# Softmax steps from VectorE to GpSimd, other decoding scratch and a new first-block order in a convolution and gated-MLP kernel

## The chip, the core and the metric

The kernel runs on one core of a Trainium2 chip. The metric is the device time of one execution in microseconds (us). The kernel before took 734.68 us (median of three executions: 734.12, 734.68 and 738.72).

## What is computed

```python
# x (4, 4160, 192), weight_gen (4, 4160, 8, 7), moe_w_in (192, 1024), moe_conv_w (3, 1024), moe_w_out (1024, 192)
w = softmax(weight_gen, axis=-1)                    # 7 taps for each token and head, 1e-9 added to the sum
x_pad = 6 zero rows ahead of each sequence, then x
a[b, s, head h] = sum over k of w[b, s, h, k] * x_pad[b, s + k, head h]      # 8 heads of 24 channels
hid = relu(a @ w_in)                                # (4, 4160, 1024)
conv = conv_w[0] * hid[s - 1] + conv_w[1] * hid[s] + conv_w[2] * hid[s + 1]  # by channel, zeros outside
out = (hid * sigmoid(conv)) @ w_out                 # (4, 4160, 192), float32
```

The weights arrive as float64, so as pairs of 32-bit words; the kernel makes float32 of them itself (the decoding below).

## The kernel before, in words

**Tiling.** The 16640 tokens lie as 128 partitions of 130 consecutive tokens. A block is four tokens of every partition, 512 in all; there are 33 blocks, and the softmax weights are loaded and normalised for a group of two blocks at a time (17 groups; group 0 holds block 0 alone, so group g holds blocks 2g-1 and 2g).

**A block** passes through these stages. *Taps* (`tap`, L283): seven products of the rows in `ring` with the softmax weights `w`, four into a tile `px` and three into `py`. *Folds*: for blocks 3 and later a DMA on POOL's queue adds `py` onto `px` (`fold1`, L314), a second one adds half of `px` onto the rest (`fold2`, L317), and POOL adds the last two (`fold3`, L321). Blocks 0 to 2 skip the folds: their seven taps are transposed one by one and summed in PSUM, and `PLAN` says for each tap whether VectorE (V) or GpSimd (G) makes it. *Transposes* (`transposes`, L326): PE turns the 192 channels onto partitions, 128 in a first part and 64 in a second; both parts of a folded block go through the same PSUM bank, so the second waits until ACT (L337) and DVE (L342) have split the first into a high and a low float32r part. *Units*: eight per block (f = 0 to 7), each five matmuls (L358), then on ACT relu (L364) and the middle conv term (L368), on DVE the two side terms (L375), on ACT the tanh (L382), on DVE the gating product (L391). Five PSUM banks hold units. *Output*: four tiles per block (L404), each eight products of float32 (16 matmul records in the trace), copied by ACT (L413) and stored.

**Softmax** (`sm_ops`): maximum on DVE (L238), subtraction (L241), exp on ACT (L244), sum on DVE (L247), 1e-9 on ACT (L251), reciprocal on DVE (L256), product (L263). `SMX` names for each group the engine of the subtraction and of the product, and `SMR` those of the groups past its end.

**Decoding** at the start: `CH` has five chunks of the first weight matrix and `WOE` four of the output weights. Each takes two ACT copies of the raw words (L132, L135), a clamp, a shift, a sign and a join (L139 to L150), and for the first matrix a split (L586, L591). Its scratch is two buffers `scr` of three slots. A chunk of kind "f" (the last 64 channels) ends in scratch, from where eight DMAs in all, the *spreads* (L603), take it to `wi`; in the kernel before the third chunk writes the same slot of `scr` as the first.

**Order.** Every step is a task with a modelled duration; a list scheduler (L786 to L849) places all of them from priorities (`TO`, `FO`, `WO_`, `FORD`), and the program is written out in the order of the placed starts. So each engine runs a fixed order, and waits in it. Around a DVE step of kind "VK" the planner keeps POOL free: before the next POOL step DVE and POOL write a small `tok` tile (L860, L861), and POOL waits for DVE there.

Of the kernel before, what the change touches and what calls it, by code (L numbers as in the profile page):

```python
# [22 lines left out]
    ("a", "GVVGGGG"),  # L23
    ("a", "GGVGGGG"),
    ("a", "GVVGVGG"),
)
REST = ("d", G7)
SMX = ("VV", "VV", "VG", "VG", "VG", "GV", "GV", "GV", "VV", "VV", "VV")
SMR = "GG"
TO = -3.05  # L30
FO = -0.55
WO_ = 1.42
NX = 3
# [7 lines left out]
    ("f", 0, 256, 5.2, "VVS", "V"),  # L41
    ("m", 0, 256, 8.7, "VGS", "V"),
    ("f", 256, 512, 17.0, "VVP", "G"),
    ("m", 256, 512, 16.0, "VVP", "V"),
    ("m", 512, 1024, 18.0, "VVP", "V"),
)
FORD = (2, 3, 5, 7, 0, 6, 1, 4)
WOE = ("VVP", "VVP", "GVS", "GVS")

# [15 lines left out]
def kernel(  # L65
# [357 lines left out]
    with tc.manual_schedule():  # L423
# [38 lines left out]
        for j in range(2, WB):  # L462
            load_w(j)
        for c in range(4):
            nc.sync.dma_start(
                out=r_out[c].rearrange("p (c d) b -> p c (d b)", c=2),
                in_=w_out.bitcast(I32)[2 * c * P:2 * (c + 1) * P, :].rearrange("(c p) e -> p c e", p=P),
            )

        temps = [hrow(f, 0, R).bitcast(I32) for f in range(2)] + [t[:, i] for t in scr for i in range(3)]  # L470

# [34 lines left out]
        def arrive(t):  # L506
            return task("none", t, [])
# [64 lines left out]
        spreads = []  # L572
        w_rdy, free = {f: [] for f in range(NF)}, {0: [], 1: []}
        for c, (kind, a, b, t, eng, wle) in enumerate(CH):
            n = b - a
            tA, tB, tC = temps[2 + 3 * (c % 2):5 + 3 * (c % 2)]
            d3 = tA[:, 0:n]
            raw = (r_in if kind == "m" else r_fold)[:, a:b, :]
            pm = eng[2] == "P"
            j_, bits = dec(None if pm else d3, raw, tB[:, 0:n], tC[:, 0:n], arrive(t), free[c % 2], eng)  # L580
            if kind == "m":
# [13 lines left out]
            if kind == "m":  # L595
                for f in range(a // P, b // P):
                    w_rdy[f].append(b_)
            else:
                def spread(th=th, a=a, b=b, n=n):
                    for s_ in range(2):  # L600
                        for r in range(2):
                            c_ = s_ * FF // 2
                            nc.sync.dma_start(  # L603
                                out=wi[r * D2:(r + 1) * D2, :, 1, c_ + a:c_ + b].bitcast(F32),
                                in_=th[s_ * D2:(s_ + 1) * D2, :, 0:n].bitcast(F32),
                            )
                b_ = dma(2.6, [b_], spread)
                spreads.append(b_)
                for f in range(a // P, b // P):
                    w_rdy[f].append(b_)  # L610
                    w_rdy[f + NF // 2].append(b_)
            free[c % 2] = [b_]
        wo_rdy = []
        for c in range(4):
            w = 2 * D
            j_, _ = dec(
                wo[:, 2 * c:2 * c + 2].rearrange("p c d -> p (c d)").bitcast(I32), r_out[c],
                temps[2 + 3 * (c % 2)][:, 0:w], temps[3 + 3 * (c % 2)][:, 0:w], arrive(21.0 + 1.5 * c), free[c % 2], WOE[c],
            )
            free[c % 2] = [j_]  # L620
            wo_rdy.append(j_)
# [72 lines left out]
        def unit(j, f):  # L694
# [11 lines left out]
            t_ = task("A", act(m_) + 0.02, [cv_], lambda: sig(j, f))  # L706
            dep = [tiles[j - 2, i] for i in range(geom(j - 2)[0])] if j >= 2 else free[0] + free[1] if j else []
            rd[n] = gm[n] = task("V", vec(m_, 0), [t_] + dep, lambda: gmul(j, f))
# [185 lines left out]
```

## Time and profile before

| what | value |
|---|---|
| median of three executions | 734.68 us |
| profiled execution | 738.26 us, span 736.3 us |
| PE busy | 697.9 us (95% of the span) |
| DVE busy | 640.1 us (87%) |
| ACT busy | 547.3 us (74%) |
| POOL busy | 497.2 us (68%) |
| mean granted TensorE clock | 0.988 of full |

The span runs from the first to the last instruction of the profiled execution; its time is 1.96 us longer. Busy shares are means over the whole span: where PE stands still is seen only by place, in the timeline and in the list of waits. The profile's line numbers are those of the kernel before; the changed kernel has the same lines one further on up to L466, and 9 to 14 further on behind that.

### The profile page before, as it was taken

To read this page: it belongs to the slowest core of one execution; us is meant where nothing else is said; L and a number is where in the kernel's file an instruction comes from. 1 tells how busy PE (TensorE), PEld (TensorE's weight loads), DVE (VectorE), ACT (ScalarE), POOL (GpSimd) and SP (SyncE) were. 2 spreads that over 40 slices of the span, in tenths; PEclk is the share of its full clock that TensorE was granted. 3 is DMA by queue.
4 is the path that set the end of the run, shared out by engine and by line. 5 is a ranking of instruction groups with operands and counts; after the bars stand their busy time and mean duration, and the time that the engine had idled before them with its cause. 6 is when DMAs were issued, how large, how long until landed. Compare 5 with 4: busy or idle time off the path is not lost.

```text
span 736.3 us, 10944 instructions
## 1 busy us (share of the span) xinstructions
PE 697.9 (95%) x3809; PEld 633.6 (86%) x3809; DVE 640.1 (87%) x1000; ACT 547.3 (74%) x1049; POOL 497.2 (68%) x391
## 2 busy tenths in 40 slices
PE   1599999999979999999999999999899999999998
PEld 1477999998979999999988999999799999999998
DVE  6589999999999998989879897979988888888882
ACT  3278788777778877868778877868687777877872
POOL 3495987989677686787778787777767887630000
PEclk9899999999999999999999999999999999999999
DMA  7615999899988867989697977889687886782111
GB/s 228 175 37 141 208 229 199 182 237 205 228 184 201 182 180 182 204 180 210 164 214 155 207 191 183 186 193 208 161 194 165 190 184 163 168 175 80 64 51 44
DMA packets 70787, 127.59 MB, mean 173 GB/s; under 512 B 5046, under 2 KB 42573, under 8 KB 70732
## 3 DMA queue, kind: packets, MB, share of 16 engines
q0 software_dynamic: 20160, 58.99, 45.5%
q1 hardware_dynamic: 50090, 67.51, 28.2%
q8 instruction: 30, 0.49, 0.3%
q10 hardware_dynamic: 482, 0.40, 0.2%
q14 instruction: 25, 0.20, 0.1%
HBM read 20.51 MB, written 12.78 MB: 45 GB/s over the span
## 4 chain that ended last, share of the span: by engine, by line
PE 28%; DMA 27%; POOL 26%; DVE 10%; issue 6%; ACT 2%; SPq 1%; POOLq 0%; DVEq 0%
DMA px<-py 23%; PE ops L404 15%; POOL py L291 12%; PE z L358 12%; POOL px L291 9%; DVE z L375 6%; POOL px L317 3%; DVE g L391 2%; POOL px L321 1%; DMA px<-px 1%; PE tp L326 1%; DMA ring<-in_x_dram 1%; ACT z L382 1%; DMA wi<-scr 1%; DMA stage<-in_moe_w_in_dram 1%
## 5 line engine op out<-in xcount | busy, mean ns | idle before, releaser
L375 DVE SCALAR_TENSOR_TENSOR z<-h,cw,z 128x512 f32<-128x512 f32 (+1 forms) x528 | 378.5, 741 | 10.3 <-ACT z L368 5.4
L404 PE MATMUL ops<-wo,g 128*128 128x192 f32 x2048 | 356.3, 328 | 0.0
L404 PEld LDWEIGHTS ops<-wo,g 128*128 128x128 f32 x2048 | 340.7, 191 | 8.5 <-DVE H L342 0.4
L358 PE MATMUL z<-H,wi 128*128 128x512 f32 x1056 | 301.7, 408 | 0.9 <-DVE g L391 0.9
L291 POOL TENSOR_TENSOR px<-ring,w 128x768 f32<-128x768 f32 (+1 forms) x142 | 225.2, 1737 | 34.1 <-PE tp L326 33.9
L358 PEld LDWEIGHTS z<-H,wi 128*128 128x128 f32 x1056 | 193.7, 189 | 36.2 <-DVE g L391 2.5
L382 ACT ACTIVATE z<-z 128x512 f32<-128x512 f32 (+1 forms) x264 | 152.1, 576 | 91.8 <-DVE z L375 89.6
L391 DVE SCALAR_TENSOR_TENSOR g<-z,h 128x512 f32<-128x512 f32 (+1 forms) x264 | 177.4, 679 | 37.8 <-ACT z L382 34.2
L364 ACT ACTIVATE h<-z 128x512 f32<-128x512 f32 x264 | 155.9, 592 | 38.4 <-PE z L358 38.0
L368 ACT ACTIVATE z<-h,cw 128x512 f32<-128x512 f32 (+1 forms) x264 | 180.0, 683 | 5.3
L291 POOL TENSOR_TENSOR py<-ring,w 128x768 f32<-128x768 f32 (+2 forms) x108 | 168.7, 1832 | 0.0
L358 PE MATMUL z<-L,wi 128*128 128x512 f32 x264 | 103.0, 390 | 0.0
L317 POOL DMA_DIRECT2D px<-px x30 | 37.4, 1248 | 74.0 <-DMA px<-py 73.6
L321 POOL TENSOR_TENSOR px<-px 128x768 f32<-128x768 f32 x30 | 66.8, 2226 | 7.0 <-DMA px<-px 7.0
L358 PEld LDWEIGHTS z<-L,wi 128*128 128x128 f32 x264 | 49.7, 188 | 10.9
L326 PE MATMUL tp<-ident,px 128*128 128x128 f32 (+1 forms) x288 | 45.3, 282 | 13.0 <-DVE L L342 10.0
L326 PEld LDWEIGHTS tp<-ident,px 128*128 128x128 f32 (+1 forms) x288 | 34.4, 132 | 20.5 <-DVE L L342 11.3
L413 ACT ACTIVATE o<-ops 128x192 f32<-128x192 f32 x128 | 41.6, 325 | 7.9 <-PE ops L404 7.6
L314 POOL DMA_DIRECT2D px<-py x30 | 40.5, 1349 | 7.6 <-POOL py L291 7.3
L337 ACT ACTIVATE H<-tp 128x512 fp32r<-128x512 f32 (+1 forms) x63 | 37.2, 591 | 5.8 <-PE tp L326 4.9
L861 POOL MEMSET tok<- 128x1 f32 x18 | 3.0, 166 | 41.0 <-DVE tok L860 41.0
L342 DVE TENSOR_TENSOR L<-tp,H 128x512 fp32r<-128x512 f32 x33 | 22.8, 689 | 7.4 <-ACT H L337 6.6
(82 smaller groups left out, 203.3 us busy)
## 6 DMA issues: line engine op xcount, KB each, us to landing
px<-py POOLq DMA_DIRECT2D x30, 1152.0 KB, 10.3
h<-h SPq DMA_DIRECT2D x128, 256.0 KB, 4.7
px<-px POOLq DMA_DIRECT2D x30, 768.0 KB, 6.6
ring<-in_x_dram SPq DMA_DIRECT2D x31, 384.0 KB, 8.2
out_dram<-o SPq DMA_DIRECT2D x31, 384.0 KB, 3.9
w<-in_weight_gen_dram SPq DMA_DIRECT2D x15, 224.0 KB, 6.9
r_out<-in_moe_w_out_dram SPq DMA_DIRECT2D x4, 384.0 KB, 6.8
wi<-scr SPq DMA_DIRECT2D x8, 128.0 KB, 3.2
```

Of the source, the lines that this page charges most:

```text
L291: eng.tensor_tensor(out=dst[:, a:b, :].rearrange("p s (h g) -> p s h g", g=GRP), in0=ring[:, p:p + n, :].rearrange("p s (h g) -> p s h g", ...
L317: nc.gpsimd.dma_start(out=fl4(px_t[q][:, 0:2]), in_=fl4(px_t[q][:, 2:4]), accum_op=ALU.add, max_dma_last_dim=3072)
L321: nc.gpsimd.tensor_tensor(out=a, in0=a, in1=b, op=ALU.add)
L326: nc.tensor.matmul(dst[0:D2 if part else P, c * P:(c + 1) * P], lhsT=src[:, c, part * P:part * D2 + P], rhs=ident, is_transpose=True, star ...
L358: nc.tensor.matmul(out=z, lhsT=w[:, fs], rhs=h_t[j, nm], start=(i == 0), stop=(i == len(terms) - 1))
L364: nc.scalar.activation(out=hrow(f, 2, R), in_=z_t[j, f], func=ACTF.Relu)
L368: nc.scalar.activation(out=z_t[j, f][:, :no * P], in_=hrow(f, cc, no), func=ACTF.Copy, scale=cw[:, NF + f:NF + f + 1])
L375: nc.vector.scalar_tensor_tensor(out=z, in0=hrow(f, cc + d, no), scalar=cw[:, k * NF + f:k * NF + f + 1], in1=z, op0=ALU.mult, op1=ALU.add,)
L382: nc.scalar.activation(out=z, in_=z, func=ACTF.Tanh, scale=0.5)
L391: nc.vector.scalar_tensor_tensor(out=g_of(j, f), in0=z_t[j, f][:, :no * P], scalar=1.0, in1=hrow(f, cc, no), op0=ALU.add, op1=ALU.mult)
L404: nc.tensor.matmul(out=ps[:, 0:D], lhsT=g_of(j, f)[:, i * P:(i + 1) * P], rhs=wo[:, f, :], start=(f == 0), stop=(f == NF - 1),)
L413: nc.scalar.activation(out=o_t[j][:, i, :], in_=ps[:, 0:D], func=ACTF.Copy, scale=0.5)
```

## The change

Six tables and the scratch differ. `SMX` is cut to four groups, so from group 4 on both softmax steps are POOL's: it gets nine more steps (the subtraction of groups 4 and 8 to 10, the product of groups 5 to 10, less that of group 2, which goes to DVE), and DVE four subtractions and five products less. `SL` gives each chunk its own slots, so that the third chunk does not write the slot that the first chunk's spread reads; the temporaries are tracked slot by slot (`last_use`). The second chunk joins on DVE and is split on POOL, the fourth is decoded in SBUF instead of PSUM. The requests for the output weights (`load_out`) become tasks behind both spreads: on SP's queue the four of them move from ahead of the first spread to behind the second one, and also behind one `ring` load and the load of group 4's weights, which waits for POOL's last tap of block 0. `PLAN`, `FORD`, `FO` and `WO_` change the engines of the first taps, the order of the first units and the priorities.

```diff
@@ -21,15 +21,15 @@
 G7 = "G" * 7
 PLAN = (
     ("a", "GVVGGGG"),
-    ("a", "GGVGGGG"),
-    ("a", "GVVGVGG"),
+    ("a", "GVVGGGG"),
+    ("a", "GVVGGGG"),
 )
 REST = ("d", G7)
-SMX = ("VV", "VV", "VG", "VG", "VG", "GV", "GV", "GV", "VV", "VV", "VV")
+SMX = ("VV", "VV", "VV", "VG")
 SMR = "GG"
 TO = -3.05
-FO = -0.55
-WO_ = 1.42
+FO = -0.65
+WO_ = 1.47
 NX = 3
 NY = 2
 NZ = 5
@@ -39,13 +39,14 @@
 CG = 2
 CH = (
     ("f", 0, 256, 5.2, "VVS", "V"),
-    ("m", 0, 256, 8.7, "VGS", "V"),
-    ("f", 256, 512, 17.0, "VVP", "G"),
-    ("m", 256, 512, 16.0, "VVP", "V"),
+    ("m", 0, 256, 8.7, "VVS", "G"),
+    ("f", 256, 512, 17.0, "GGP", "G"),
+    ("m", 256, 512, 16.0, "VVS", "V"),
     ("m", 512, 1024, 18.0, "VVP", "V"),
 )
-FORD = (2, 3, 5, 7, 0, 6, 1, 4)
-WOE = ("VVP", "VVP", "GVS", "GVS")
+FORD = (1, 3, 2, 7, 0, 6, 5, 4)
+SL = ((0, 1, 2), (3, 4, 5), (1, 0, 2), (4, 3, 5), (1, 4, 5))
+WOE = ("VGP", "VGP", "GVS", "GVS")
 
 
 def vec(n, ps=1):
@@ -461,13 +462,15 @@
             load_in(nc.sync, *c[:3])
         for j in range(2, WB):
             load_w(j)
-        for c in range(4):
+
+        def load_out(c):
             nc.sync.dma_start(
                 out=r_out[c].rearrange("p (c d) b -> p c (d b)", c=2),
                 in_=w_out.bitcast(I32)[2 * c * P:2 * (c + 1) * P, :].rearrange("(c p) e -> p c e", p=P),
             )
 
-        temps = [hrow(f, 0, R).bitcast(I32) for f in range(2)] + [t[:, i] for t in scr for i in range(3)]
+
+        temps = [hrow(f, 0, R).bitcast(I32) for f in range(2)]
 
         def run(steps):
             for s_ in steps:
@@ -570,14 +573,20 @@
 
 
         spreads = []
-        w_rdy, free = {f: [] for f in range(NF)}, {0: [], 1: []}
+        w_rdy, last_use = {f: [] for f in range(NF)}, {i: [] for i in range(6)}
+        slots = [t[:, i] for t in scr for i in range(3)]
+
+        def used(ix):
+            return [k for i in ix for k in last_use[i]]
+
         for c, (kind, a, b, t, eng, wle) in enumerate(CH):
             n = b - a
-            tA, tB, tC = temps[2 + 3 * (c % 2):5 + 3 * (c % 2)]
+            iA, iB, iC = SL[c]
+            tA, tB, tC = slots[iA], slots[iB], slots[iC]
             d3 = tA[:, 0:n]
             raw = (r_in if kind == "m" else r_fold)[:, a:b, :]
             pm = eng[2] == "P"
-            j_, bits = dec(None if pm else d3, raw, tB[:, 0:n], tC[:, 0:n], arrive(t), free[c % 2], eng)
+            j_, bits = dec(None if pm else d3, raw, tB[:, 0:n], tC[:, 0:n], arrive(t), used(SL[c][pm:]), eng)
             if kind == "m":
                 hi, lo = wh[:, 0, a:b], wl[:, 0, a:b]
             else:
@@ -595,6 +604,8 @@
             if kind == "m":
                 for f in range(a // P, b // P):
                     w_rdy[f].append(b_)
+                for i_ in SL[c][pm:]:
+                    last_use[i_] = [b_]
             else:
                 def spread(th=th, a=a, b=b, n=n):
                     for s_ in range(2):
@@ -604,20 +615,23 @@
                                 out=wi[r * D2:(r + 1) * D2, :, 1, c_ + a:c_ + b].bitcast(F32),
                                 in_=th[s_ * D2:(s_ + 1) * D2, :, 0:n].bitcast(F32),
                             )
+                for i_ in SL[c][pm:]:
+                    last_use[i_] = [b_]
                 b_ = dma(2.6, [b_], spread)
+                last_use[iB] = [b_]
                 spreads.append(b_)
                 for f in range(a // P, b // P):
                     w_rdy[f].append(b_)
                     w_rdy[f + NF // 2].append(b_)
-            free[c % 2] = [b_]
         wo_rdy = []
         for c in range(4):
             w = 2 * D
+            iB, iC = ((1, 2), (4, 5))[c % 2]
             j_, _ = dec(
                 wo[:, 2 * c:2 * c + 2].rearrange("p c d -> p (c d)").bitcast(I32), r_out[c],
-                temps[2 + 3 * (c % 2)][:, 0:w], temps[3 + 3 * (c % 2)][:, 0:w], arrive(21.0 + 1.5 * c), free[c % 2], WOE[c],
+                slots[iB][:, 0:w], slots[iC][:, 0:w], dma(1.6, spreads, lambda c=c: load_out(c)), used((iB, iC)), WOE[c],
             )
-            free[c % 2] = [j_]
+            last_use[iB] = last_use[iC] = [j_]
             wo_rdy.append(j_)
 
 
@@ -704,7 +718,7 @@
             cv_ = task("V", vec(m_), [y_], lambda: conv_side(j, f, 2, 1))
             cv_ = task("V", vec(m_), [cv_], lambda: conv_side(j, f, 0, -1))
             t_ = task("A", act(m_) + 0.02, [cv_], lambda: sig(j, f))
-            dep = [tiles[j - 2, i] for i in range(geom(j - 2)[0])] if j >= 2 else free[0] + free[1] if j else []
+            dep = [tiles[j - 2, i] for i in range(geom(j - 2)[0])] if j >= 2 else wo_rdy if j else []
             rd[n] = gm[n] = task("V", vec(m_, 0), [t_] + dep, lambda: gmul(j, f))
             zl.append(gm[n])
             f0 = f // CG * CG
```

What the scheduler makes of it is shown at three places. First DVE, where the third chunk is decoded (`dps` is its PSUM bank, `scr_107` the scratch of the first chunk, `scr_108` the other one). Before:

```order
L263 TENSOR_TENSOR w<-w,r 128x448 [waits DVE_49]
L860 MEMSET tok_102 128x1
L139 TENSOR_SCALAR dps<-dps 128x256 [waits Activation_49]
L142 TENSOR_SCALAR scr_107<-dps 128x256 [waits DMAHW2_49,DMAHW1_49,DMAHW7_49,DMAHW0_49,DVE_49]
L145 SCALAR_TENSOR_TENSOR dps<-dps,scr_107 128x256 [waits DVE_49]
L268 TENSOR_TENSOR w<-w,edge 128x168
L860 MEMSET tok_103 128x1
```

And now:

```order
L264 TENSOR_TENSOR w<-w,r 128x448 [waits DVE_49]
L140 TENSOR_SCALAR scr_108<-scr_108 128x256 [waits Activation_49]
L269 TENSOR_TENSOR w<-w,edge 128x168 [waits DVE_49]
L140 TENSOR_SCALAR dps<-dps 128x256 [waits Activation_49]
L874 MEMSET tok_101 128x1
L143 TENSOR_SCALAR scr_107<-dps 128x256 [waits DVE_49]
L146 SCALAR_TENSOR_TENSOR dps<-dps,scr_107 128x256 [waits DVE_49]
L143 TENSOR_SCALAR scr_108<-scr_108 128x256 [waits Pool_49]
L239 TENSOR_REDUCE m<-w 128x64 [waits DMAHW1_49]
L874 MEMSET tok_102 128x1
L239 TENSOR_REDUCE m<-w 128x64 [waits DMAHW2_49]
L151 ISA dps<-dps,scr_107 128x512 [waits DVE_49,Activation_49]
```

The shift into `scr_107` no longer waits for DMAs, and the clamp and shift of the fourth chunk and two maxima of the softmax stand ahead of the tokens that release POOL.

Second POOL, around the subtraction for group 5 (`w_637` before, `w_631` now) and the block that is folded there; the tokens and DMAs of earlier blocks are as printed. Before:

```order
L291 TENSOR_TENSOR py_1045<-ring_98,w_145 128x768 x2
L314 DMA px_983<-py_1045 128x3x768 [waits Pool_49]
L241 TENSOR_TENSOR w_637<-w_637,m_958 128x448 [waits DMAHW7_49]
L321 TENSOR_TENSOR px_865<-px_865 128x768 [waits DMASW5_49]
L291 TENSOR_TENSOR px_983<-ring_98,w_145 128x768
```

And now:

```order
L292 TENSOR_TENSOR py_1195<-ring_98,w_333 128x768 x2
L315 DMA px_1146<-py_1195 128x3x768 [waits Pool_49]
L242 TENSOR_TENSOR w_631<-w_631,m_961 128x448 [waits DMAHW7_49]
L242 TENSOR_TENSOR w_857<-w_857,m_1143 128x448 [waits DMAHW0_49,DVE_49]
L322 TENSOR_TENSOR px_983<-px_983 128x768 [waits DMASW7_49]
```

The subtraction stands behind the first fold of block 7 (`px_1146`) instead of block 6 (`px_983` in both), and that of group 6 follows it at once.

Third PE, between the two parts of a folded block's transposes (block 9, `px_1462` before and `px_1511` now). Before:

```order
L326 MATMUL tp_1947<-ident_91,px_1462 128x128 x3
L358 MATMUL z_1956<-H1_1779,wi_95 128x512 x2
L358 MATMUL z_1956<-H2_1781,wi_95 128x512 x2
L358 MATMUL z_1956<-L1_1780,wi_95 128x512
L358 MATMUL z_1971<-H1_1779,wi_95 128x512 [waits DVE_49]
L358 MATMUL z_1971<-H1_1779,wi_95 128x512
L358 MATMUL z_1971<-H2_1781,wi_95 128x512 x2
L358 MATMUL z_1971<-L1_1780,wi_95 128x512
L326 MATMUL tp_1982<-ident_91,px_1462 64x128 [waits DVE_49]
```

And now:

```order
L327 MATMUL tp_1902<-ident_91,px_1511 128x128 x3
L359 MATMUL z_1907<-H1_1725,wi_95 128x512 [waits DVE_49]
L359 MATMUL z_1907<-H1_1725,wi_95 128x512
L359 MATMUL z_1907<-H2_1727,wi_95 128x512 x2
L359 MATMUL z_1907<-L1_1726,wi_95 128x512
L405 MATMUL ops_1920<-wo_96,g_1709 128x192 [waits Activation_49]
L405 MATMUL ops_1920<-wo_96,g_1709 128x192 x6
L405 MATMUL ops_1920<-wo_96,g_1709 128x192 [waits DVE_49]
L327 MATMUL tp_1940<-ident_91,px_1511 64x128 [waits DVE_49]
```

One unit and one output tile stand between the two parts, where two units stood. In the kernel before 19 of the 30 folded blocks have two units there, 10 two units and a tile, and one a unit and a tile; now 27 have a unit and a tile, blocks 3 and 4 a tile alone, and block 5 two units.

## Rows read from the trace of the kernel before

**Rows 1.** The page, PE busy in 40 slices of the span, in tenths

```profile
PE   1599999999979999999999999999899999999998
```

**Rows 2.** Chain that ended last, two pieces of it: start us, us, what

```profile
557.56 2.28 PE z L358 x10
...
559.84 2.60 PE ops L404 x16
```

**Rows 3.** Timeline of the start: start us, us, engine, line, operation [idle before, releaser]

```profile
26.41 0.43 DVE L142 TENSOR_SCALAR scr<-dps 128x256 int32<-128x256 int32 x1 [6.32 <-DMA wi<-scr]
...
29.16 4.54 POOL L291 TENSOR_TENSOR px<-ring,w 128x768 f32<-128x768 f32 x3
...
29.26 1.11 PE L326 MATMUL tp<-ident,py 128*128 128x128 f32 x4 [6.71 <-POOL py L291]
...
34.59 1.15 DVE L241 TENSOR_TENSOR w<-w,m 128x448 f32<-128x448 f32 x2
...
35.52 1.18 PE L358 MATMUL z<-H,wi 128*128 128x512 f32 x4
```

**Rows 4.** Timeline, DVE's tokens and the transposes of block 2

```profile
37.09 0.06 DVE L860 MEMSET tok<- 128x1 f32 x1
...
61.34 0.66 PE L326 MATMUL tp<-ident,px 128*128 128x128 f32 x4 [0.23 <-DVE px L291]
...
62.98 0.06 DVE L860 MEMSET tok<- 128x1 f32 x1
```

**Rows 5.** Timeline: blocks 3, 4, 9 on POOL and PE; exp of group 5

```profile
68.10 1.44 POOL L314 DMA_DIRECT2D px<-py  x1 [0.32 <-POOL py L291]
...
104.03 2.33 POOL L321 TENSOR_TENSOR px<-px 128x768 f32<-128x768 f32 x1
...
108.76 0.60 PE L326 MATMUL tp<-ident,px 128*128 128x128 f32 x4
...
129.83 0.57 ACT L244 ACTIVATE w<-w 128x448 f32<-128x448 f32 x1
...
189.95 2.30 POOL L321 TENSOR_TENSOR px<-px 128x768 f32<-128x768 f32 x1
...
206.74 0.60 PE L326 MATMUL tp<-ident,px 128*128 128x128 f32 x4
```

**Rows 6.** Timeline around the stop of PE at 210 us

```profile
208.54 1.83 POOL L321 TENSOR_TENSOR px<-px 128x768 f32<-128x768 f32 x1 [0.20 <-DMA px<-px]
...
208.57 2.28 DVE L263 TENSOR_TENSOR w<-w,r 128x448 f32<-128x448 f32 x1
...
213.36 0.89 PE L326 MATMUL tp<-ident,px 128*64 128x128 f32 x4 [3.72 <-DVE L L342]
```

**Rows 7.** Timeline around the stop of PE at 524 us

```profile
522.42 2.11 DVE L260 TENSOR_SCALAR r<-r,mask 128x8 f32<-128x8 f32 x1
...
527.31 0.82 PE L326 MATMUL tp<-ident,px 128*64 128x128 f32 x4 [2.95 <-DVE L L342]
```

**Rows 8.** Stretches: us, busy us (x) by engine, granted clock, DMA share, GB/s

```profile
140.00:180.00 40.00, 39.53 (x217) 35.83 (x216) 38.15 (x57) 29.30 (x58) 36.99 (x28) 1.00 1.01 214
...
213.60:217.00 3.40, 3.40 (x14) 3.36 (x13) 3.31 (x6) 2.86 (x5) 3.08 (x3) 0.50 1.07 186
```

**Rows 9.** Groups by line and shape (busy us, mean ns); L375: ns min/median/max

```profile
L241 POOL TENSOR_TENSOR w<-w,m 128x448 f32<-128x448 f32 x9 | 12.2, 1357 | 0.0
...
L263 DVE TENSOR_TENSOR w<-w,r 128x448 f32<-128x448 f32 x7 | 8.6, 1225 | 0.0
...
L375 DVE SCALAR_TENSOR_TENSOR z<-h,cw,z x528: 474/750/757, 38.7 to 720.4; 128x512 f32<-128x512 f32 x170, 128x256 f32<-128x256 f32 x6
```

**Rows 10.** Waits of PE: engine, line <- releaser: us in total, times, longest

```profile
PE tp L326 <- DVE L L342: 10.0, 6, 3.7
```

**Rows 11.** Timeline around a late softmax step at 380 us

```profile
380.22 0.58 ACT L244 ACTIVATE w<-w 128x448 f32<-128x448 f32 x1 [3.75 <-POOL w L241]
...
382.28 0.63 PE L326 MATMUL tp<-ident,px 128*64 128x128 f32 x4 [0.95 <-DVE L L342]
```

## The prediction

> **What bounds the kernel now.** I read the busy slices of the page first. PE is full in nearly every slice behind the first three [rows 1], so the time is PE's own work plus the places where PE stands still, and only what happens there can move it. The chain of waits gives the price of the work: two units take 2.28 us and an output tile 2.60 us [rows 2]. A block of eight units and four tiles is then 4 x 2.28 + 4 x 2.60 = 19.52 us, and no engine change alters that. Next I went through the timeline for the stops. There are three large ones. At the start PE waits 6.71 us for a tap of POOL, which waits for DVE, which has waited 6.32 us until the spread had read its scratch [rows 3]. At 210 us PE waits 3.72 us and at 524 us 2.95 us, both for DVE's split between the two parts of a block's transposes [rows 6, 7]. Behind the stop at 210 us the granted clock is 0.50 for the 3.40 us of its stretch [rows 8], which is the lower level, 1.2 GHz; work done there costs up to 1.7 us more. I take 1.4 us for each of the two stops. Smaller waits for the same split make up the rest of a total of 10.0 us [rows 10].
>
> Why the split is late differs in origin and not in kind. At 208.57 us DVE's softmax product takes 2.28 us, while POOL's third fold runs from 208.54 to 210.37 [rows 6]; the mean of the seven such products is 1.225 us [rows 9]. At 522.42 us a multiplication of only eight columns takes 2.11 us [rows 7]. The conv steps of DVE, which take one operand from PSUM, stay between 0.474 and 0.757 us in all 528 cases [rows 9]. So some DVE steps on SBUF alone wait for a POOL step to finish, and the ordinary ones do not. The Trainium skill (SBUF — State Buffer, section "SBUF: two separate sides") says of the port pair that VectorE and GpSimd share that whichever starts first holds it for its whole instruction; the trace agrees.
>
> **The change part by part**, against the profiled execution's own 738.26 us (span 736.3 us, 1.96 us beside it).
>
> *Start.* Without the wait DVE goes on at 26.41 - 6.32 = 20.09 us. The new order puts more ahead of the token for POOL's last tap of block 0: nine steps of about 0.43 us as the shift at 26.41, some already counted before 20.09, and two subtractions, 1.15 us together [rows 3]. From the softmax product's end at about 19.7 us that is 19.7 + 3.9 + 1.15 = 24.8 us, and up to 0.6 us more if the subtractions wait for POOL's tap. The last tap then starts near 25.3 us instead of 29.16 us [rows 3]: 3.9 us earlier. The first unit stands at 35.52 us [rows 3], 6.4 us behind that tap, and follows it as before; the three groups of transposes that it now overtakes come after it and give nothing. PE's long pause shrinks to pauses below 2 us, so the transposes may run at 0.66 us as in rows 4 and not at 1.11 us as in rows 3: four groups, overlapped, perhaps 0.6 us. I take 4.5 us; the range is 2.5 (a blocked subtraction, half clock) to 6.0 (nearly the whole wait).
>
> *First blocks on DVE.* From DVE's token at 37.09 us to that at 62.98 us it decodes, runs block 0's conv and makes taps, with PE waiting for one of them at 61.34 us [rows 4]. The list behind the new token is shorter by one tap and a reciprocal and longer by a clamp: nothing to speak of, 25.9 us again. So the 4.5 us are carried to 61.34 us, and neither more nor less is taken for it. The output weights are asked for behind the load that waits for POOL's last tap of block 0, so about 28 us if that tap starts at 25.3 us. Their first copy on ACT follows the decode of the fifth chunk, which begins at DVE's token (37.09 - 4.5 = 32.6 us [rows 4]) and shares DVE with block 0's conv, so some 6 us later. That leaves 10 us for the load. I cost it at nothing, under the cover of that decode; if the cover fails, see the last rival.
>
> *Blocks 3 to 6 on POOL.* POOL gains less than PE. One tap of block 3 has moved behind the token at 62.98 us, so the first fold at 68.10 us [rows 5] comes only about 3 us earlier. Before, the third fold of block 4 ended at 106.4 us (104.03 + 2.33) for transposes at 108.76 us [rows 5], 2.4 us ahead. In the new PE order two units and a tile more stand ahead of these transposes, 4.88 us [rows 2], so PE arrives at 108.76 + 4.88 - 4.5 = 109.1 us; POOL's order puts a second fold, two taps and a subtraction more ahead of that third fold, and it ends at 108 to 110 us. Then the exp for group 5: before at 129.83 us, with nothing to wait for [rows 5]. Now its subtraction stands behind the first fold of block 7, near 128 us, and ACT reaches the exp near 126 us. A wait of 3.75 us at such an exp cost PE 0.95 us [rows 11]. I take -1.5 us for both; from 0 to -5 (one stop with its half clock).
>
> *The softmax steps.* POOL has nine steps more of about 1.4 us [rows 9]. From block 6 on they lie beside slack: at block 9 the third fold ended at 192.25 us for transposes at 206.74 us [rows 5]. DVE loses the product that collided at 208.57 us. With it go 3.72 + 1.4 = 5.1 us; I keep 0.2 us back: **4.9 us**.
>
> *The stop at 524 us.* Its DVE step stays (the mask of the last group). But it now lies in the middle of a block, and between the two parts PE has a unit and a tile, 1.14 + 2.60 = 3.74 us, where it had two units, 2.28 us [rows 2]. The stop was 2.95 + 1.4 = 4.35 us; I take 4.0 us, from 0 to 4.4.
>
> *The small waits* for the split: 10.0 - 3.72 - 2.95 = 3.3 us [rows 10], of which some 0.7 at the start. By the longer cover I take 1.0 us, from 0 to 2.5.
>
> Sum: 4.5 - 1.5 + 4.9 + 4.0 + 1.0 = 12.9 us. 738.26 - 12.9 = **725.4 us**. The profiled execution is 3.6 us above the median shown, 734.68 us; I think one of the two stops can be missing in an execution, so against the median the gain is 9.3 us, 1.3%.
>
> **The rivals.**
>
> *POOL is late in blocks 4 to 6* (0.20). For it: POOL has 36.99 of 40 us busy between 140 and 180 us [rows 8], and its margin at block 4 was 2.4 us. Then one stop with half clock takes 5.2 us instead of 1.5: 738.26 - 4.5 + 5.2 - 4.9 - 4.0 - 1.0 = 729.1 us.
>
> *The stops only move* (0.15). POOL's steps are longer than those they replace, the fixed order can bring another DVE step on SBUF or a late exp to the same place, and 4.9 and 4.0 us are not won: 734.3 us. For it: the wait of ACT in rows 11 is of a group whose steps are already POOL's. Against it: the two stops apart, PE waited for the split only 3.3 us in the whole run [rows 10], though POOL made both steps of six groups. The Trainium skill (Perfetto Trace Analysis, section "Optimizing Scalar/DVE Operations") says that moving work between VectorE and GpSimd may not help because they share a read port; by that rule alone it would be this rival's time. The trace bears it out for DVE steps on SBUF alone, of which hardly any are left.
>
> *POOL becomes the bound* (0.06). Nine steps of 1.4 us are 12.6 us before block 20, most of them where POOL is at 92% [rows 8]. If POOL's lead stays below zero from block 4 to block 9 (it was 14.5 us at block 9 [rows 5]), PE waits at each of six blocks, 12.6 us in all, and each wait brings its half clock, 6 x 1.4 = 8.4 us: 738.26 - 4.5 - 4.9 + 12.6 + 8.4 = 749.9 us; half of that is 744 us. It decides where the third fold of block 6 ends later than PE's arrival. The output weights would join it if they came more than 10 us after they are asked for: ACT and DVE would wait in order for them.
>
> That the change doesn't do what it says is left out: the wait on the DMAs is gone from the shift in the printed order. The rest, 0.03, is open.
>
> **How the numbers follow.** My forecast has 0.56. What this measurement tells from no change is about 1%, 7.3 us: below 727.3 us is faster, above 742.0 us slower. With the bounds of its terms the forecast reaches from 719 to 731 us, and about four fifths of it lie below 727.3 (0.45); of the first rival a third (0.07), of the second a tenth (0.02). So faster 0.54, same 0.40, slower 0.06. The range takes in the first two rivals and leaves a tenth at either end: 719.5 to 734.5 us.
>
> **What would show it.** The start: no wait of DVE for the spread, block 0's last tap near 25 us, the first unit near 30 us, DVE's token near 58 us. POOL: the third fold of block 4 between 108 and 110 us, the exp of group 5 waiting 1 to 3 us. The middle: no wait of PE above 1 us between 140 and 520 us, and a granted clock of 1.00 there. At the mask step DVE may still take 2 us, but PE must not stop. I am wrong if DVE's time at the start is taken by a new wait, if PE stops for a fold in blocks 4 to 6, or if stops of 3 us stand elsewhere.

## The result and the profile after

The changed kernel takes **724.04 us** (median of 4 runs, 722.55 to 725.42) where the one before takes 734.86 us (median of 4, 734.12 to 738.72): ratio 0.9842, 95% interval 0.9802 to 0.9882. The forecast was 725.4 us. The profiled execution took 722.55 us (span 720.8 us) where that of before took 738.26: 15.7 us are gone, and my sum had 12.9. Medians against medians it is 10.8 us, where I had 9.3. The execution traced before is among the longest of its kernel (granted clock 0.988) and the one traced after is the shortest of its four (0.998), so the 15.7 us are more than the change is worth.

The page's slices answer to [rows 1]; the second row is the granted clock in tenths.

```profile
PE   2799999899999999999999999999999999999998
...
PEclk9999999999999999999999999999999999999999
```

PE is full from the third slice on, and no slice behind the second falls below 8. The timeline of the start answers to [rows 3, 4].

```profile
13.72 3.19 SPq L614 DMA_DIRECT2D wi<-scr  x4
...
20.70 0.42 DVE L143 TENSOR_SCALAR scr<-dps 128x256 int32<-128x256 int32 x1
...
23.86 1.90 DVE L242 TENSOR_TENSOR w<-w,m 128x448 f32<-128x448 f32 x2
...
25.90 3.05 POOL L292 TENSOR_TENSOR px<-ring,w 128x768 f32<-128x768 f32 x2
...
29.86 1.97 SPq L467 DMA_DIRECT2D r_out<-in_moe_w_out_dram  x4
...
30.40 2.05 PE L359 MATMUL z<-H,wi 128*128 128x512 f32 x4
...
56.93 0.06 DVE L874 MEMSET tok<- 128x1 f32 x1
```

DVE's shift (20.70) no longer waits; block 0's last tap starts at 25.90 us (it was 29.16), the first unit at 30.40 (35.52), DVE's token stands at 56.93 us (62.98). Next, from the same timeline, blocks 4 to 6 and the mask step, which answer to [rows 5, 7].

```profile
106.49 1.85 POOL L322 TENSOR_TENSOR px<-px 128x768 f32<-128x768 f32 x1
...
108.39 0.66 PE L327 MATMUL tp<-ident,px 128*128 128x128 f32 x4
...
128.91 2.39 POOL L242 TENSOR_TENSOR w<-w,m 128x448 f32<-128x448 f32 x2
...
130.41 0.58 ACT L245 ACTIVATE w<-w 128x448 f32<-128x448 f32 x1 [4.28 <-POOL w L242]
...
132.25 1.21 PE L359 MATMUL z<-H,wi 128*128 128x512 f32 x4 [2.25 <-DVE g L392]
...
501.19 0.35 DVE L261 TENSOR_SCALAR r<-r,mask 128x8 f32<-128x8 f32 x1
```

The third fold of block 4 ends at 108.34 us for transposes at 108.39: just in time. POOL's subtractions at 128.91 us are late for ACT's exp, and PE stops 2.25 us: the only stop above 1.2 us behind the first unit. The mask step took 0.35 us and not 2.11. The waits (us in total, times, longest) answer to [rows 10]:

```profile
ACT w L245 <- POOL w L242: 10.2, 7, 4.3
...
PE z L359 <- DVE g L392: 3.4, 2, 2.2
...
PE tp L327 <- DVE L L343: 1.1, 1, 1.1
```

Two stretches, columns as in [rows 8]:

```profile
132.20:135.80 3.60, 3.55 (x17) 3.10 (x18) 3.48 (x6) 3.49 (x8) 3.60 (x4) 1.00 1.06 186
140.00:180.00 40.00, 40.00 (x221) 36.62 (x221) 39.11 (x60) 32.43 (x63) 34.09 (x27) 1.00 0.88 204
```

The clock is 1.00 in both, and PE's waits for the split fell from 10.0 us to 1.1, although ACT now waits 10.2 us for POOL's subtractions (6.9 us before).

### The profile page after: what moved, and what is told of

Same layout as the page of the kernel before. It is cut to its first block, busy times and chain, and to the rows that moved or that the text cites. A ratio compares the mean times of both kernels' runs of the same rounds, so it can differ in the third digit from the quotient of the medians.

```text
span 720.8 us, 10895 instructions
## 1 busy us (share of the span) xinstructions
PE 693.8 (96%) x3809; PEld 630.0 (87%) x3809; DVE 633.2 (88%) x981; ACT 546.9 (76%) x1049; POOL 503.8 (70%) x390
## 4 chain that ended last, share of the span: by engine, by line
PE 82%; POOL 10%; DMA 4%; issue 2%; DVE 1%; ACT 1%; SPq 0%; POOLq 0%
PE ops L405 41%; PE z L359 36%; POOL py L292 4%; POOL px L292 4%; PE tp L327 3%; DMA px<-py 2%; DMA ring<-in_x_dram 1%; POOL px L318 1%; PE z L405 1%; DMA stage<-in_moe_w_in_dram 1%; POOL px L322 0%; POOL px L315 0%; DVE px L292 0%; POOL w L242 0%; SPq L437 0%
## 5 line engine op out<-in xcount | busy, mean ns | idle before, releaser
L405 PEld LDWEIGHTS ops<-wo,g 128*128 128x128 f32 x2048 | 338.8, 190 | 10.2 <-DVE H L343 0.4
L292 POOL TENSOR_TENSOR px<-ring,w 128x768 f32<-128x768 f32 (+2 forms) x141 | 229.6, 1774 | 66.8 <-PE tp L327 66.5
L392 DVE SCALAR_TENSOR_TENSOR g<-z,h 128x512 f32<-128x512 f32 (+1 forms) x264 | 179.5, 681 | 34.7 <-ACT z L383 32.0
L315 POOL DMA_DIRECT2D px<-py x30 | 42.7, 1424 | 6.4 <-POOL py L292 6.3
L343 DVE TENSOR_TENSOR H<-tp,H 64x512 fp32r<-64x512 f32 x30 | 20.5, 683 | 2.2 <-ACT H L338 1.3
```

The lines of the kernel that those rows point to most:

```text
L292: eng.tensor_tensor(out=dst[:, a:b, :].rearrange("p s (h g) -> p s h g", g=GRP), in0=ring[:, p:p + n, :].rearrange("p s (h g) -> p s h g", ...
L343: nc.vector.tensor_tensor(out=H[D2:P, :] if part else h_t[q, "L1"], in0=tp[r, :], in1=H[r, :].bitcast(F32), op=ALU.subtract)
L392: nc.vector.scalar_tensor_tensor(out=g_of(j, f), in0=z_t[j, f][:, :no * P], scalar=1.0, in1=hrow(f, cc, no), op0=ALU.add, op1=ALU.mult)
L405: nc.tensor.matmul(out=ps[:, 0:D], lhsT=g_of(j, f)[:, i * P:(i + 1) * P], rhs=wo[:, f, :], start=(f == 0), stop=(f == NF - 1),)
```

## The experiments

They were timed in three groups, each beside the kernel before on one chip. The three parts alone and the single product stood beside 736.29 us (median of 23 runs); positions and softmax steps of before, and the two runs with subtractions on DVE, beside 735.86 us (7); the wait put back, the changed kernel once more and the two runs with other planned durations beside 736.59 us (7). Ratios are to those, with their 95% interval in brackets. I call *cover* the work that PE has between the two parts of a block's transposes: two units (2.28 us) in most blocks before, a unit and a tile (3.74 us) in most blocks now.

### The three parts, each alone

**Start alone**: the change's `CH`, `FORD`, `SL`, `WOE`, `PLAN`, slots and late `load_out`; shown as an edit of the changed kernel.

```
-SMX = ("VV", "VV", "VV", "VG")
+SMX = (as before, eleven groups)
-FO = -0.65; WO_ = 1.47
+FO = -0.55; WO_ = 1.42
```

> The scratch, the late request of the output weights and the first blocks' engines of the change, with the softmax steps and the two positions (FO, WO_) of before. My theory: the start is worth 7.2 us by itself (PE's lost time at the work in front of block 3 is 34.5 us before and 27.3 us after), and nothing later gives it back: some 727.5 us against 734.7, with stops of 3 to 5 us left in the middle wherever DVE's split is late. Rival: POOL is what limits blocks 3 to 6, so a start that is earlier for PE alone is lost again before 110 us at a wait for a third fold: 731 us or more, and PE loses 3 us or more between 60 and 135 us.

730.72 us, ratio 0.9922 [0.9893, 0.9951]: 5.6 us, where the theory had 7.2; the time is nearer to the rival's. Stops remain. The largest, in the timeline:

```profile
290.30 0.58 ACT L245 ACTIVATE w<-w 128x448 f32<-128x448 f32 x1 [3.04 <-POOL w L242]
...
292.87 0.63 PE L327 MATMUL tp<-ident,px 128*64 128x128 f32 x4 [3.17 <-DVE L L343]
```

No DVE product is involved: ACT, in order, waited 3.04 us at an exp, its copy of the transposes came late, and so did DVE's split. Between 60 and 135 us PE lost 2.1 us at two third folds (0.8 at 89.08 us, 1.4 at 108.67), where it lost 0.4 before: of the rival's 3 us, two thirds. The stops of before at 213 and 527 us are both gone, although this kernel keeps the softmax steps and the cover of before. Its seven softmax products on DVE took 0.73 us on average, and the mask step was not blocked (busy us, mean ns):

```profile
L261 DVE TENSOR_SCALAR r<-r,mask 128x8 f32<-128x8 f32 x1 | 0.2, 228 | 0.0
```

**Softmax steps alone** (before, with the new `SMX`).

> Only the softmax steps from the fifth group on go to POOL; start and positions as before. My theory: the stop at 210 us goes (5.1 us with its half clock), the stop of the last group's mask step stays if its step again falls on a POOL step (4.4 us), and a late exp near 130 us costs 0 to 2.5 us: 730 to 732 us. Rival (the stops only move): another DVE step on SBUF or a late exp brings the same 5 us elsewhere: 735 us, with a stop of PE above 2 us between 100 and 400 us.

733.20 us, 0.9963 [0.9942, 0.9984]: 3.1 us, between theory and rival. The stop at 210 us is gone, and so is that at the mask step, which took 0.23 us here. The rival came true later in the run (timeline):

```profile
336.29 0.58 ACT L244 ACTIVATE w<-w 128x448 f32<-128x448 f32 x1 [3.22 <-POOL w L241]
...
338.86 1.06 PE L326 MATMUL tp<-ident,px 128*64 128x128 f32 x4 [3.91 <-DVE L L342]
```

The stretch behind it, columns as in [rows 8]:

```profile
338.80:342.30 3.50, 3.44 (x13) 3.33 (x14) 3.47 (x7) 2.96 (x6) 2.29 (x2) 0.50 1.01 227
```

With two units (2.28 us) between the parts, a late exp makes the same kind of stop as a slow product, and behind it the granted clock was 0.50, the lower level.

**Positions alone** (before, with `FO = -0.65`, `WO_ = 1.47`).

> Only the two positions FO and WO_ are changed: PE now has a unit and an output tile (3.74 us) between the two parts of every later transpose, where it had two units (2.28 us) or two units and a tile. My theory: cover decides. The DVE products on SBUF still collide with POOL and take about 2.2 us, but PE's wait for the split shrinks from 3.7 and 3.0 us to 0 to 2 us: a gain of 4 to 7 us, 728 to 731 us, and the wait of PE for the split (10.0 us in all before) falls below 5 us. Rival: where the step falls beside POOL's decides, and the cover does not: the wait for the split stays above 7 us and the time is 735 us, or the exp of one group is late and takes it back.

732.25 us, 0.9951 [0.9936, 0.9965]: 4.0 us, and the wait for the split 4.5 us in all, as the theory had it. In the timeline:

```profile
174.03 6.51 POOL L291 TENSOR_TENSOR px<-ring,w 128x768 f32<-128x768 f32 x4
...
176.08 4.95 DVE L263 TENSOR_TENSOR w<-w,r 128x448 f32<-128x448 f32 x1
...
190.94 0.63 PE L326 MATMUL tp<-ident,px 128*64 128x128 f32 x4 [1.72 <-DVE L L342]
...
210.79 1.60 DVE L263 TENSOR_TENSOR w<-w,r 128x448 f32<-128x448 f32 x1
...
213.04 0.62 PE L326 MATMUL tp<-ident,px 128*64 128x128 f32 x4 [1.46 <-DVE L L342]
```

DVE stood 4.95 us at one product, and PE did not stop for it: no transposes were due then. At 210.79 us a product takes 1.60 us, and the stop behind it is 1.46 us where it was 3.72. The mask step took 0.37 us here too, so the stop of before at 527 us is missing for a reason other than the cover.

### One collision taken away

Before, with only the ninth group's product on POOL.

```
-SMX = (..., "GV", "GV", "GV", "VV", "VV", "VV")
+SMX = (..., "GV", "GV", "GV", "VG", "VV", "VV")
```

> As before, with one step moved: the softmax product of the ninth group (the one that takes 2.28 us on DVE at 208.57 us, in front of the stop) is POOL's. My theory: that collision alone made the stop, so the stop of 3.7 us and its half clock go, 5 us: 730 us, with the stop of the mask step still there. Rival: DVE is late there from its own queue, and the split stays late by 2 us or more: 734 to 735 us, PE still waits about 3 us near 213 us.

733.97 us, 0.9960 [0.9936, 0.9985], and the stop stands where it was, longer, in its timeline:

```profile
201.73 3.06 DVE L241 TENSOR_TENSOR w<-w,m 128x448 f32<-128x448 f32 x1
...
213.78 0.83 PE L326 MATMUL tp<-ident,px 128*64 128x128 f32 x4 [4.10 <-DVE L L342]
```

My theory fell: the product at 208.57 us was not the only reason for a late split. Another step on SBUF alone, a subtraction, now collides 7 us ahead, and DVE carries the delay to the transposes: from 201.73 to 213.78 us it stood idle for 0.23 us in all. Where the 2.3 us come from can be seen elsewhere in the trace. PE's wait for the split behind 100 us is 6.8 us and was 9.3: the stop of 2.95 us at the mask step is gone, and one of 2.03 us has come at 299.43 us. The mask step's row (busy us, mean ns):

```profile
L260 DVE TENSOR_SCALAR r<-r,mask 128x8 f32<-128x8 f32 x1 | 0.4, 416 | 0.0
```

### The changed kernel with one part undone

**Positions of before**: `FO = -0.55`, `WO_ = 1.42`.

> The changed kernel with the two positions FO and WO_ of before; PE has 2.28 us between many pairs of transposes again. Theory A (the cover is what keeps the stops away, since in the three kernels with the old cover a late exp of POOL's groups or a slow DVE step made a stop of 2 to 4 us each): PE waits for the split 5 to 10 us in all again, the granted clock falls behind at least one stop, 728 to 731 us. Theory B (the softmax steps on POOL take the stops away, and the cover adds its own 4 us elsewhere): the sum of the parts, 736.3 - 5.6 - 3.1 = 727.6 us or less, with a wait for the split of 3 us or less.

728.98 us, 0.9920 [0.9889, 0.9951]: theory A. PE's wait for the split is 6.7 us again, and in the timeline one stop again has a lower clock behind it:

```profile
251.73 0.63 PE L327 MATMUL tp<-ident,px 128*64 128x128 f32 x4 [2.41 <-DVE L L343]
```

The stretch behind it:

```profile
251.70:255.10 3.40, 3.37 (x16) 3.37 (x17) 3.30 (x6) 2.85 (x5) 2.66 (x2) 0.71 1.03 173
```

The 0.71 is a mean: up to 253.1 us the clock was 1.00, from 253.2 to 256.5 us it was 0.50.

**Softmax steps of before**: the old `SMX`.

> The changed kernel with the softmax steps of before (DVE again makes 8 steps more between the third and the eleventh group). Theory A (the cover of 3.74 us absorbs DVE's slow steps): the move of the softmax steps is worth little on top of the cover, 723 to 725 us, DVE products of 1.6 to 2.3 us are there and PE waits for the split 3 us or less; the stop of 2.2 us at 130 us may go. Theory B (the moves add up as the parts do): 736.3 - 5.6 - 4.0 = 726.7 us or more, with stops of 1.5 to 2 us where a product collides with a POOL step.

727.03 us, 0.9887 [0.9853, 0.9921]: theory B, and its timeline shows why.

```profile
214.45 5.76 DVE L264 TENSOR_TENSOR w<-w,r 128x448 f32<-128x448 f32 x1
...
214.73 4.99 POOL L292 TENSOR_TENSOR py<-ring,w 128x768 f32<-128x768 f32 x3
...
225.81 0.63 PE L327 MATMUL tp<-ident,px 128*64 128x128 f32 x4 [2.73 <-DVE L L343]
```

The stretch behind this stop, in the same columns:

```profile
225.80:229.00 3.20, 3.19 (x17) 2.77 (x18) 3.17 (x6) 2.55 (x6) 0.41 (x2) 1.00 1.10 181
```

A product of 0.62 us stood 5.76 us, until POOL's run of three taps was over at 219.72 us; that is more than a cover of 3.74 us holds. Mean of the seven products here: 1.97 us. Not all that this kernel loses is the product's: in the same trace PE waits 2.20 us for a third fold at 86.34 us and 1.58 us for a tap at 55.73 us.

**The wait for the spread put back**: one entry of the slot table.

```
-SL = ((0, 1, 2), (3, 4, 5), (1, 0, 2), (4, 3, 5), (1, 4, 5))
+SL = ((0, 1, 2), (3, 4, 5), (0, 1, 2), (4, 3, 5), (1, 4, 5))
```

> The changed kernel with one table entry undone: the third chunk is decoded into the scratch that the spread of the first still reads, so the wait for the transfer is back and nearly nothing else in the order moves. Theory (the wait is what the start gains): DVE waits 5 to 6 us for the spread, POOL's last tap of block 0 starts near 31 us instead of 25.90, the first unit near 36 us instead of 30.40, and all of it stays on the path: 724 + 5.5 to 7 = 729.5 to 731 us. Rival (the order of the first blocks does it: engines, FORD, steps pulled ahead): DVE has other work or POOL has slack, and the time is 726 us or less.

723.80 us, 0.9831 [0.9803, 0.9859]: the theory fell, outright. In its timeline the wait is 1.23 us where it was 6.32 [rows 3]:

```profile
13.81 15.42 SPq L614 DMA_DIRECT2D wi<-scr  x8
...
22.00 0.43 DVE L143 TENSOR_SCALAR scr<-dps 128x256 int32<-128x256 int32 x1 [1.23 <-DMA wi<-scr]
...
30.40 1.97 SPq L467 DMA_DIRECT2D r_out<-in_moe_w_out_dram  x4
```

The kernel before, on the same queue:

```profile
14.01 2.82 SPq L465 DMA_DIRECT2D r_out<-in_moe_w_out_dram  x4
...
16.95 3.69 SPq L603 DMA_DIRECT2D wi<-scr  x4
```

The spread stood on SP behind four requests for the output weights, 2.82 us of issuing; it is now asked for 3.1 us earlier and has read its source 4.4 us earlier (22.00 against 26.41 us). The scratch of its own is worth nothing that shows. That the place of the requests makes the difference is read from these rows; the late request alone, on the kernel before, was not run.

### Where the remaining stop can go

**Changed kernel, once more**, unchanged.

> The changed kernel once more, unchanged, beside the other three: 722 to 726 us, and a profile whose stop near 130 us (2.2 us, behind a late exp) and whose missing stops near 210 and 510 us are the same if they belong to the order, and differ if they are chance.

723.74 us, 0.9836 [0.9801, 0.9870]; again one stop, 2.25 us at 132.45 us, behind the same exp, and none near 210 or 510 us. It belongs to the order.

**The sixth group's subtraction on DVE**: `SMX = ("VV", "VV", "VV", "VG", "GG", "VG")`.

> The changed kernel with one subtraction, that of the sixth group, on DVE, which in the changed kernel POOL makes at 128.91 us, late by 4.28 us for ACT's exp. If that wait makes PE's stop at 130 us, the stop (2.25 us) goes and the time is 721.5 to 722.5 us; rival: the next group's subtraction or another step of POOL is late in its place, PE stops 1.5 us or more between 110 and 160 us, 724 us.

727.24 us, 0.9883 [0.9850, 0.9915]: the rival, and worse than it. The stop at 130 us is gone; the order behind it fell otherwise, and in the timeline the next late exp meets a pair of transposes:

```profile
284.49 0.58 ACT L245 ACTIVATE w<-w 128x448 f32<-128x448 f32 x1 [5.41 <-POOL w L242]
...
286.37 1.06 PE L327 MATMUL tp<-ident,px 128*64 128x128 f32 x4 [2.81 <-DVE L L343]
```

**The sixth and seventh on DVE.**

> The changed kernel with the subtractions of the sixth and the seventh group on DVE (in the changed kernel POOL makes both in a row behind 128.91 us). The same question as with one: if POOL is late for the seventh group too, this gives 721 to 722 us and no stop of PE above 1 us between 100 and 160 us; rival: two subtractions on DVE collide with POOL's steps (up to 2 us each instead of 0.62) and PE stops for the split: 724 us or more.

727.18 us, 0.9893 [0.9860, 0.9925]: the same, with waits for the split of 2.4 us at 185 us and 1.3 us at 290 us. One of the two subtractions took 5.47 us on DVE (169.53 us), beside POOL's run of three taps that ended at 174.51 us: more than the 2 us that the rival had.

**POOL's softmax steps planned 0.5 us longer** (`pool(N) + 0.5` in the planner's cost, 1.65 us).

> The changed kernel with one planner's cost changed: a softmax step of POOL counts 0.5 us more, 1.65 us, as the trace shows (mean 1.63 and 1.42 us), where it counted 1.15. Theory (stops come from exps that ACT reaches before POOL has finished, because POOL is planned too fast): ACT's wait for POOL's subtraction falls from 10.2 us to below 6 us, the stop near 130 us goes, 720 to 722 us. Rival (the other costs of POOL, 250 taps planned at 1.5 us and measured at 1.8, set how late it is; and the order falls otherwise by chance): no gain, 723 to 727 us, with a stop of 2 us or more at another place.

724.96 us, 0.9848 [0.9822, 0.9873]. ACT's wait for POOL fell to 0.8 us in all and the stop at 130 us went, as the theory had it; the time did not follow, as the rival had it. A row of PE's timeline:

```profile
89.07 1.12 PE L327 MATMUL tp<-ident,px 128*128 128x128 f32 x4 [2.74 <-POOL px L322]
```

Now PE waits for a third fold of POOL, and the list of waits has none of PE behind 100 us.

**More of POOL's steps planned longer** (also `1.78` to `2.25` for the third fold, taps of 1.5 us to 1.8 us from the fifth block on; the 1.8 us is a mean over whole and partial taps, and the whole ones alone, 128x768, took 1.90 and 1.96 us in the changed kernel).

> As the previous one, and also the third fold planned at 2.25 us (it was 1.78; the trace's mean is 2.28) and the taps from the fifth block on at 1.8 us (they were 1.5; the means are 1.77 and 1.85). Theory: with POOL planned as slow as it is, ACT waits less than 4 us for POOL's subtractions in all and PE has no stop of 1.5 us or more behind 100 us: 719 to 722 us. Rival: POOL's plan is now too slow, its steps come early and fold or tap are late instead, or the order falls otherwise by chance: 723 to 728 us.

722.23 us (721.68 to 724.24), 0.9815 [0.9786, 0.9844]: the lowest of all, though from the changed kernel's 0.9836 it can't be told, and the time lies between those of theory and rival. ACT waits for no subtraction of POOL any more, as the theory had it; but behind 60 us one stop is left in the timeline, at a third fold again, which the theory did not have:

```profile
101.74 1.81 POOL L322 TENSOR_TENSOR px<-px 128x768 f32<-128x768 f32 x1 [0.99 <-DMA px<-px]
...
103.60 0.66 PE L327 MATMUL tp<-ident,px 128*128 128x128 f32 x4 [2.09 <-POOL px L322]
```

The stretch behind it:

```profile
103.60:107.00 3.40, 3.40 (x14) 3.40 (x15) 2.40 (x4) 2.29 (x4) 3.40 (x3) 0.58 1.02 231
```

This 0.58 is a mean too: from 104.2 to 107.5 us the clock was 0.50.

## Why the prediction was right, and where it was not

To size the terms I counted PE's work up to a point (1.14 us a unit, 2.60 a tile, 0.44 for four transposes) and took it from the time of that point; what is left is what PE had lost by then. It is good to about 1 us.

| stretch | term forecast | PE lost, before | PE lost, after | gained |
|---|---|---|---|---|
| to the first unit (35.52, now 30.40 us) | +4.5 | 27.3 | 23.5 | 3.8 |
| from there to block 3 (69 us) | 0 | 6.4 | 4.1 | 2.3 |
| from there to 199 us, now 196 | -1.5 | 0.9 | 3.7 | -2.8 |
| from there to 241 us, now 235 | +4.9 | 5.7 | 0.0 | 5.7 |
| from there to 521 us, now 503 | +1.0 | 2.7 | 0.6 | 2.1 |
| from there to 547 us, now 542 | +4.0 | 4.8 | 0.0 | 4.8 |
| the rest | 0 | 0.2 | 0.5 | -0.3 |

The last column sums to 15.6 us; the two spans differ by 15.5. The table compares two executions, and the medians differ by 10.8 us (12.9 when it was timed again), so some of its rows are larger than the change makes them on average; which ones, no second trace of the kernel before shows.

That 725.4 us came so near to 724.04 is in part luck: the sum was 2.7 us short of what the traces show, and it was taken from an execution 3.4 us above the median of the kernel before.

*Start: right in kind, too small, and put down to the wrong edit.* Block 0's last tap and the first unit came 0.6 and 0.4 us later than I had them, so up to there 3.8 us came of 4.5. What failed is the step "neither more nor less is taken" for the first blocks on DVE. Before, PE had a stop there that I did not put into the sum (timeline of the kernel before):

```profile
42.80 1.05 PE L326 MATMUL tp<-ident,py 128*128 128x128 f32 x4 [1.33 <-POOL py L291]
43.50 2.05 PE L358 MATMUL z<-H,wi 128*128 128x512 f32 x4
```

The same stretch of before, columns as in [rows 8]:

```profile
42.80:46.30 3.50, 3.50 (x11) 2.91 (x12) 1.79 (x4) 0.86 (x3) 3.50 (x3) 0.52 0.09 34
```

It waited 1.33 us for a tap, and behind that the granted clock was 0.52, so the unit took 1.86 us instead of 1.14. In the changed kernel the transposes of that block wait 0.41 us at most, and the clock is 1.00 from 40.40 to 43.90 us: that is about the size of the 2.3 us. And the wait that I read as the scratch's is not the scratch's: with the old slot back it was 1.23 us and the time the same. By the rows it went with the place of four requests in SP's queue, a move that I had costed at nothing.

*Blocks 3 to 6: right in place, low in size.* The third fold of block 4 was forecast to end between 108 and 110 us and ended at 108.34; the exp of the sixth group (group 5 of the prediction) was to wait 1 to 3 us and waited 4.28. So -2.8 us, not -1.5. The half clock that I allowed for did not come: the stretch from 132.20 us has 1.00.

*The softmax steps: right in size, not in reason.* The stop went. But the run that took only its product away kept a stop of 4.10 us, so that collision was not necessary for the stop; and with the start alone the stop was gone with the product still DVE's, so the move was not necessary to end it. What the move does is shown by the changed kernel without it: seven products of 1.97 us on average, one of 5.76, and 3.3 us more (727.03 against 723.74; the intervals overlap).

*The stop at 524 us: right in size, by another way.* I kept the slow mask step and trusted the cover. In the changed kernel it met only the end of a tap, 0.35 us, and the cover was not called on there. Nor was it in any other kernel measured here: the step took 0.22 to 0.42 us in each of them, also in the three with the cover of before that changed the start alone, the softmax steps alone or one product. So that stop stood in the one order of the kernel before, and the gain of each part alone holds its end. That the cover works is shown elsewhere, by the runs with the positions alone and without them: 4.0 and 5.2 us, the second free of the mask step.

*The small waits* gave 2.1 us where I took 1.0; the range went to 2.5.

*The rivals.* "POOL is late in blocks 4 to 6" half came true, at half its price. "The stops only move" did not for the whole change, but it is what the softmax steps do alone (a stop of 3.91 us at 339 us) and what each repair of the last stop did. The Trainium skill (Perfetto Trace Analysis, section "Optimizing Scalar/DVE Operations") says that moving work between VectorE and GpSimd might not help. The runs show both cases: with the cover of before and the new start nothing shows of it (0.9920 with the move, 0.9922 without), with the longer cover it gave 3.3 us, though the intervals overlap.

*The parts together.* Alone they give 5.6, 3.1 and 4.0 us, 12.7 together; the whole gave 10.8 and 12.9 us. The sums agree, but not because the parts are independent. PE's wait for the split behind 100 us, in us, by kernel:

| | softmax steps of before | softmax steps of the change |
|---|---|---|
| cover of before | 9.3 (kernel before), 4.9 (start alone) | 8.1 (softmax alone), 6.1 (positions of before) |
| cover of the change | 3.8 (positions alone), 3.4 (softmax steps of before) | 0.0 (changed kernel, both times), 0.5 (wait put back) |

These are single traces, and of the 9.3 us the mask step's stop is 2.95, so 6.4 are left to compare. The cover lowers the wait in either column (6.4 to 3.8, 4.9 to 3.4, 6.1 to 0.0). The softmax steps end what is left under the longer cover (3.4 to 0.0) and show no such effect without it (6.4 to 8.1, 4.9 to 6.1). The corner with the whole start undone and the two others kept was not run, so what the start is worth beside them is not shown.

## What to carry to other kernels

A stop of the bound engine has an owner only in one order: before you credit an edit with it, undo that edit alone, since the same wait may hang on a request queued ahead of another. A stop that rests on two engines meeting by chance, like that at the mask step, can go with any change of the order, and every edit then seems to have earned it. Where several late steps feed one in-order chain, lengthening the cover in front of the wait helped where removing one step did not: apart from the stop at the mask step, which went in both, the wait for the split behind 100 us fell from 6.4 to 3.8 us, while removing one late step left it at 6.8 (in time 4.0 and 2.3 us were gained, with overlapping intervals). And planning a slow engine nearer to its measured durations took the waits for its subtractions from 10.2 us to none; the next step in line took over, and no gain of time could be told from the noise.

## What was not expected of the hardware

- A DVE step on SBUF alone can wait for several POOL instructions in a row: 4.95 us at 176.08 us, until four back-to-back taps ended at 180.54, 5.76 us at 214.45 us, until three ended at 219.72, and 5.47 us at 169.53 us, until three ended at 174.51; each was over about 0.5 us later. The Trainium skill (SBUF — State Buffer, section "SBUF: two separate sides") says that the first to start holds the pair for its whole instruction; measured here, POOL's next instructions came ahead of a DVE step that was already waiting, so the price was the length of POOL's run.
- The length of a stop alone does not tell whether TensorE's clock falls behind it. Two stops of nearly the same length, 2.74 us (longer planned softmax steps, 89.07 us) and 2.73 us (softmax steps of before, 225.81 us), were followed by 0.50 and 1.00 of the clock; behind 3.91 and 2.09 us it fell to 0.50, behind 2.41 us it did so 1.4 us later, and behind 2.25 us it stayed at 1.00. At the start, behind the same two waits of 1.61 and 1.07 us, it was 0.50 from 29.2 to 32.6 us in the traced execution of the changed kernel and 1.00 in that of the run with the wait put back.
